# Double-to-single weight words: four VectorE steps or three, and where ScalarE's word lies

## Chip, core and metric

One NeuronCore of one Trainium2 chip. Its engines each take their own instructions in program order: TensorE (PE, matrix products, with a separate weight load PEld), VectorE (DVE), ScalarE (ACT), GpSimd (POOL) and SyncE (SP), which here issues almost all DMAs. Matrix products are written to PSUM, eight banks of 512 single-precision columns in each of 128 partitions; DVE and ACT read and write it. The metric is the device time of one execution in microseconds (us), the median of several runs.

## What is computed

Attention with hashed buckets, and a two-layer feed-forward part on its output:

```python
q_bits = (einsum('bhsd,dk->bhsk', q, proj) > 0)          # 6 hash bits, k the same
mask = q_bucket[:, :, :, None] == k_bucket[:, :, None, :]
scores = where(mask, matmul(q, k.T) / sqrt(D), -1e9)
attn = exp(scores - max(scores)); attn /= sum(attn) + 1e-9
x = matmul(attn, v)                  # 4 batches, 8 heads, 768 rows, 64 columns -> (3072, 512)
h = x @ w_in                         # (512, 2048)
g = where(h >= 1, h, where(h <= -1, 0, (h + 1) ** 2 / 4))
out = g @ w_out                      # (2048, 512)
```

`w_in` and `w_out` come in double precision. The kernel sees each weight as two 32-bit words (low and high) and has to make the single-precision word itself: the sign, the exponent with its bias changed, and the top 23 bits of the fraction, of which 20 lie in the high word and 3 at the top of the low word.

## The kernel before

**Heads, units, queues.** There are 32 heads in 16 pairs. A head has 12 units: six blocks of 128 keys for each half of the queries (384 columns). Unit g puts out two score products (L372, L373) into a PSUM bank "s", then two exponentials on ACT: `ph` (L381) and the same again unrounded (L386), in place or, for blocks 0 and 3, in the SBUF tile `pf`. The subtraction of the two (L392, recorded at line 39 of the helper `sub`) is done one unit later, on DVE or, for blocks 0 and 3, on POOL. Four units later three products (L405, L407, L409) add the unit to the output bank: `obank[0]` while the first half of the queries runs, `obank[1]` for the second. After a half's last block ACT copies the bank to SBUF (L415). So bank 0 takes products in units 4 to 9 of a head, bank 1 in units 10 to 15, that is, up to unit 3 of the next head.

**Row maxima.** Two heads ahead, PE forms the products of the row maxima, a pair of matmuls (L311) at the end of every second unit. DVE reduces both halves at once (L315) in the next unit. There is one such two-bank tile, so the next pair of matmuls waits for the reduction. POOL clamps the finished maxima (L343, L345), PE transposes them (L350), ACT copies them (L355) and two DMAs put them away.

**Hash bits.** For the pair after next, POOL rounds the raw queries and keys and subtracts (L153, L158) in units 0 to 3 of an even head. `bits_mm` forms a hash product of four matmuls (L211) for each half and ACT negates a part of it (L217); `bits_cmp`, one unit later, compares on DVE (L222). Line 589 says at which unit and in which bank; a DMA (`move`, part 3) and POOL's scaling (`bits_scale`) are set relative to the second product, the put of the bits at unit 18.

**Weight words.** `WeightSplit.steps` returns a word's steps as closures: a load of 128 x 512 doubles (`s0`), a square on ACT and a first DVE step (`s1`), three more DVE steps (`s2`, `s3`, `s4`), then a rounding (`s5`, L87 or L89), the remainder (`s6`, POOL or DVE, line 39) and DMAs (`put`, `get`). The last DVE step uses the square to set words to zero whose exponent is too small. `conv` hangs the steps of a word on the units of a head by a tuple of offsets. Twelve words of `w_in` start with every odd head from head 3 (L1166), twelve more words (four of `w_in`, eight of `w_out`) with every even head from head 4 (L1178). The eight left are made in the feed-forward part, by steps set a given number of blocks before the word is needed (L1234).

**Order.** Nothing is reordered: the loop over the units (L614 to L636) calls a unit's score products, the reduction held over, the subtraction of the unit before, the output products, and then the tasks hung on that unit. The feed-forward loop does the same with `prep` and `post`.

Of the kernel before, what the change touches and what calls it, by code (L numbers as in the profile page):

```python
# [31 lines left out]
BIG = 2.0 ** 36  # L32
CLAMP = 2.0 ** 33
SCALE = 1.0 / 8.0
WMIN2 = float(np.array([897 << 20], np.int32).view(np.float32)[0]) ** 2


def sub(nc, eng, out, a, b):
# [3 lines left out]
class WeightSplit:  # L42
# [3 lines left out]
    def __init__(self, nc, pool, n):  # L46
        self.nc, self.pool, self.n = nc, pool, n
        sc = pool.tile([P, 2], I32, name="wsc", bufs=1)
        nc.vector.memset(sc[:, 0:1], -0x40000000)
        nc.vector.memset(sc[:, 1:2], 29)  # L50
        self.sc = sc

    def steps(self, src, shape, hi, lo, cp, stage=None, low=None, keep=None):
        nc, n = self.nc, self.n
        st = {}

        def s0():
            st["raw"] = self.pool.tile([P, n, 2], I32, name="wraw")
            dst = st["raw"]
            if len(shape) == 4:  # L60
                dst = dst.rearrange("p (c f) t -> p c f t", c=shape[1])
            nc.sync.dma_start(out=dst, in_=src)

        def s1():
            raw = st["raw"]
            sq = st["sq"] = self.pool.tile([P, n], F32, name="wsq")
            a = st["a"] = self.pool.tile([P, n], I32, name="wa", bufs=1)
            high = raw[:, :, 1].bitcast(F32)
            nc.scalar.activation(out=sq, in_=high, func=AF.Square)
            nc.vector.tensor_scalar(out=a, in0=raw[:, :, 1], scalar1=0x07FFFFFF, scalar2=3,  # L70
                                    op0=ALU.bitwise_and, op1=ALU.logical_shift_left)

        def s2():
            nc.vector.scalar_tensor_tensor(out=st["a"], in0=st["raw"][:, :, 1], scalar=self.sc[:, 0:1],
                                           in1=st["a"], op0=ALU.bitwise_and, op1=ALU.bitwise_or)

        def s3():
            nc.vector.scalar_tensor_tensor(out=st["a"], in0=st["raw"][:, :, 0], scalar=self.sc[:, 1:2],
                                           in1=st["a"], op0=ALU.logical_shift_right, op1=ALU.bitwise_or)

        def s4():
            nc.vector.scalar_tensor_tensor(out=st["sq"], in0=st["sq"], scalar=WMIN2,
                                           in1=st["a"].bitcast(F32), op0=ALU.is_ge, op1=ALU.mult)

        def s5():
            if cp is nc.scalar:
                cp.copy(out=hi, in_=st["sq"])  # L87
            else:
                cp.tensor_copy(out=hi, in_=st["sq"])  # L89

        def s6():
            sub(nc, low or nc.gpsimd, lo, st["sq"], hi.bitcast(F32))

        def put():
            nc.sync.dma_start(out=keep if stage is None else stage, in_=st["sq"])

        if stage is None:
            return [s0, s1, s2, s3, s4, s5, s6] + ([put] if keep is not None else [])

        def get(sq=None):  # L100
            st["sq"] = self.pool.tile([P, n], F32, name="wsq") if sq is None else sq
            nc.sync.dma_start(out=st["sq"], in_=stage)

        return [s0, s1, s2, s3, s4, put], [get, s5, s6]


NQK, NV, NP_ = 3, 2, 7
# [7 lines left out]
def attention(ctx, tc, wst, T1, T2, qk, v, pj, cv, x_d, s_d, e_d, tasks, shared):  # L115
# [1 line left out]
    const = ctx.enter_context(tc.tile_pool(name="aconst", bufs=1))  # L117
    work = ctx.enter_context(tc.tile_pool(name="awork", bufs=2))
    small = ctx.enter_context(tc.tile_pool(name="asmall", bufs=2))
    shared["work"], shared["small"] = work, small  # L120
    ps_s = ctx.enter_context(tc.tile_pool(name="ps_s", bufs=4, space=PSUM))
    ps_o = ctx.enter_context(tc.tile_pool(name="ps_o", bufs=1, space=PSUM))
    ps_m = ctx.enter_context(tc.tile_pool(name="ps_m", bufs=1, space=PSUM))
# [447 lines left out]
    for hd in range(NH):  # L571
        pr, h = hd // 2, hd % 2
        g = hd * NU
        if 0 < hd < NH - 2:
            gc, gt = ((30, 33), (41, 43))[hd - 1] if hd < 3 else (g + NU + SHIFT - 1, g + NU + SHIFT + 1)
            at(gc, max_clamp, hd + 2, nc.gpsimd)
            at(gt, max_tr, hd + 2)
            at(gt, max_put, hd + 2)
        if h == 0 and pr + 2 < NPAIR:
            g0 = g + (13, 2)[pr] if pr < 2 else g  # L580
            for n in range(4):
                at(g0 + n, cast_h, pr + 2, nc.gpsimd, n % 2, n // 2)
                at(g0 + n, low_h, pr + 2, nc.gpsimd, n % 2, n // 2)
            at(g0 + 3, move, pr + 2, 0)
            at(g0 + 3, move, pr + 2, 1)
            at(g0 + 6, move, pr + 2, 2)
            if pr + 3 < NPAIR:
                at(g0 + 7, load_raw, pr + 3)
            bits_at = ((20, 1), (23, 0)) if pr == 0 else ((8 if pr == 1 else 7, 1), (11, 0))
            for hf, (n, bank) in enumerate(bits_at):  # L590
                at(g + n, bits_mm, pr + 2, hf, bank)
                at(g + n + 1, bits_cmp, pr + 2, hf)
            at(g + n + 1, move, pr + 2, 3)
            at(g + n + (2 if pr else 1), bits_scale, pr + 2, nc.gpsimd if pr else nc.scalar)
            at(g + (18 if pr else 25), bits_put, pr + 2)
        if h == 0 and pr + 1 < NPAIR:
            gv = g + LAG + (2 if pr else 16)
            at(gv, cast_v, pr + 1, nc.scalar)
            at(gv + 1, split_v, pr + 1, nc.gpsimd, 0)
            at(gv + 3, split_v, pr + 1, nc.gpsimd, 1)  # L600
            if pr + 2 < NPAIR:
                at(gv + (6 if pr else 4), load_v, pr + 2)
# [503 lines left out]
def lsh_attn_ffn(ctx: ExitStack, tc: tile.TileContext, qk, v, pj, cv, w_in, w_out, out):  # L1106
# [46 lines left out]
    def conv(g, steps, offs):  # L1153
        for fn, n in zip(steps, offs):
            at(g + n, fn)

    def wi_steps(i, cp, stage=None):
        return ws.steps(win_v[:, :, i * P:(i + 1) * P, :], (P, NCT, P, 2), wih[i], wil[i], cp, stage, None, wq[i])

    def wo_steps(i, cp, stage=None, low=None):  # L1160
        return ws.steps(wout_v[i], (P, DM, 2), woh[i], wol[i], cp, stage, low)

    woh = [hi for hi, lo in wo]
    wol = [lo for hi, lo in wo]
    for i in range(NW1):
        conv((2 * i + 3) * NU, wi_steps(i, nc.scalar), (0, 7, 9, 13, 15, 17, 19, 21))  # L1166
    g0 = (NH - 4) * NU
    late = {}
    for n in range(NSTG):
        i = n - (NFT - NW1)  # L1170
        stage = wq[NW1 + n] if i < 0 else xdp.tile([P, DM], F32, name=f"wd{n}")
        if i < 0:
            first, late[n] = wi_steps(NW1 + n, nc.vector, stage)
        elif i < 2:
            first, late[n] = wo_steps(i, nc.vector, stage)
        else:
            first, late[n] = wo_steps(i, nc.scalar, stage, nc.gpsimd if i < 4 else nc.vector)
        conv((4 + 2 * n) * NU, first, (0, 7, 9, 13, 15, 16))  # L1178
    for n, g in enumerate((1, 7, 13, 25, 30, 35)):
        conv(g0 + g, late[n], (0, 5, 6))  # L1180

    actx = ExitStack()
    attn = {}
    for b in range(B - 1):
        g = (b + 1) * H * NU + LAG + 4
        at(g, lambda b=b: xm.sums_load(*(attn["small"].tile([P, NF], F32, name=n, bufs=1) for n in ("sm", "em")), b))
# [31 lines left out]
    for i in range(2, NFT):  # L1218
# [12 lines left out]
        else:  # L1231
            need -= 2 + (i > 9)
            *st, cast, low = wo_steps(i, nc.scalar, None, nc.vector)
            for fn, m in zip(st, (6, 4, 4, 3, 3)):  # L1234
                prep[need - m].append((fn, ()))
            n_cast, n_low = need - 3, need - 2
        post[n_cast].append((cast, ()))
# [53 lines left out]
```

## Time and profile before

| | us |
|---|---|
| runs (3) | 979.09, 979.32, 982.97 |
| median | 979.32 |
| profiled execution | 979.4 |
| its span | 977.6 |
| DVE busy | 788.3 |
| ACT busy | 680.2 |
| POOL busy | 354.8 |

The span is what the profiler recorded between the first and the last instruction. The granted clock of PE is 0.9 of full speed or more in every slice. Busy times are sums over instructions; PE's matmuls are pipelined, so that two of them overlap in the record and a busy PE is not a PE at its peak: the distance between the starts of neighbours says more. An idle engine that nobody waits for costs nothing.

Slices 1 to 18 of the 40 are attention, the rest the feed-forward part. The busy shares in tenths:

```profile
PE   8999999999999999999999999999999999999998
PEld 7889999999999999999999998888988888888896
DVE  8779999999999999897898788787776777655554
```

### The profile page before, as it was taken

Reading aid. Unit: us, or ns where it says so; the run is one execution under the profiler, and the core shown is the slowest. Engines: PE = TensorE matmul, PEld = TensorE weight load, DVE = VectorE, ACT = ScalarE, POOL = GpSimd, SP = SyncE. Lnnn points to the kernel's source line nnn. Section 1 sums busy time; section 2 is a strip of 40 time slices with the busy share of each in tenths; the row PEclk is TensorE's granted clock in tenths of the full one; section 3 lists DMA queues with packets and bytes.
Section 4 is the critical chain, followed back from the end, with each engine's and each line's share of the span. In section 5 each row is a group of like instructions: output and inputs, shape, how many; then the busy total and the mean of one; then the engine's idle time right before and its main releaser. Section 6 shows DMA issues by size and latency. Waiting matters only on the chain.

```text
span 977.6 us, 15547 instructions
## 1 busy us (share of the span) xinstructions
PE 961.9 (98%) x5050; PEld 890.3 (91%) x5050; DVE 788.3 (81%) x1355; ACT 680.2 (70%) x1481; POOL 354.8 (36%) x422
## 2 busy tenths in 40 slices
PE   8999999999999999999999999999999999999998
PEld 7889999999999999999999998888988888888896
DVE  8779999999999999897898788787776777655554
ACT  7888998989989998987755565455564545544444
POOL 8768887777788877566000000000000000000000
PEclk9999999999999999999999999999999999999999
DMA  5775566677666666635494479976459554454431
GB/s 161 191 183 157 153 170 177 175 191 197 179 167 166 157 175 176 153 114 134 128 335 162 139 227 300 295 241 201 119 160 236 146 183 118 148 154 119 119 87 65
DMA packets 95113, 167.56 MB, mean 171 GB/s; under 512 B 13956, under 2 KB 51960, under 8 KB 95032
## 3 DMA queue, kind: packets, MB, share of 16 engines
q1 hardware_dynamic: 94808, 166.56, 60.7%
q8 instruction: 40, 0.66, 0.3%
q14 instruction: 41, 0.34, 0.1%
q10 hardware_dynamic: 224, 0.00, 0.0%
HBM read 106.13 MB, written 33.87 MB: 143 GB/s over the span
## 4 chain that ended last, share of the span: by engine, by line
PE 86%; DVE 5%; POOL 5%; ACT 1%; issue 1%; DMA 1%; DVEq 0%; POOLq 0%; ACTq 0%
PE y L829 27%; PE h L1061 18%; PE h L966 7%; PE smax L311 6%; PE s L373 5%; PE s L372 5%; PE o L405 5%; PE o L407 5%; PE o L409 5%; POOL t L39 3%; PE o L211 2%; DVE nm L315 2%; DVE pl L39 1%; POOL pl L39 1%; POOL t L153 1%
## 5 line engine op out<-in xcount | busy, mean ns | idle before, releaser
L381 ACT ACTIVATE ph<-s 128x384 fp32r<-128x384 f32 x380 | 188.6, 496 | 41.2 <-PE s L373 36.1
L315 DVE TENSOR_REDUCE nm<-smax 128x1 f32<-128x768 f32 x189 | 179.3, 949 | 22.2 <-PE smax L311 21.0
L39 POOL TENSOR_TENSOR pl<-pf,ph 128x384 fp32r<-128x384 f32 x128 | 134.1, 1052 | 78.8 <-ACT pf L386 78.8
L794 DVE SCALAR_TENSOR_TENSOR t<-t 128x384 f32<-128x384 f32 x128 | 71.2, 557 | 101.0 <-ACT z L789 100.8
L39 DVE TENSOR_TENSOR pl<-s,ph 128x384 fp32r<-128x384 f32 x256 | 135.4, 545 | 10.9 <-ACT s L386 9.0
L372 PE MATMUL s<-t 128*128 128x384 f32 x384 | 132.2, 344 | 0.0
L373 PE MATMUL s<-t 128*128 128x384 f32 x384 | 129.6, 337 | 1.7 <-DMA t<-te 1.7
L409 PE MATMUL o<-pl,va 128*128 128x386 f32 x384 | 130.4, 340 | 0.4 <-DVE pl L39 0.4
L407 PE MATMUL o<-ph,vb 128*128 128x386 f32 x384 | 130.0, 339 | 0.0
L405 PE MATMUL o<-ph,va 128*128 128x386 f32 x384 | 129.9, 338 | 0.0
L386 ACT ACTIVATE s<-s 128x384 f32<-128x384 f32 x252 | 125.5, 498 | 0.0
L829 PE MATMUL y<-t,ghi 128*128 128x512 f32 x384 | 124.7, 395 | 0.0
L311 PE MATMUL smax<-t 128*128 128x384 f32 x378 | 100.1, 346 | 4.5 <-DVE nm L315 4.4
L788 ACT ACTIVATE t<-h,mh 128x384 f32<-128x384 f32 x56 | 32.5, 581 | 82.2 <-PE h L966 43.5
L799 ACT CAST ghi<-z 128x384 fp32r<-128x384 f32 x129 | 65.1, 505 | 30.6 <-DVE z L795 26.9
L789 ACT ACTIVATE z<-t,m 128x384 f32<-128x384 f32 x128 | 79.0, 617 | 4.2
L829 PEld LDWEIGHTS y<-t,ghi 128*128 128x128 f32 x384 | 71.3, 188 | 11.1 <-ACT ghi L799 0.3
L1061 PE MATMUL h<-wbig,t 128*128 128x384 f32 x399 | 81.4, 336 | 0.0
L311 PEld LDWEIGHTS smax<-t 128*128 128x128 f32 x378 | 66.6, 188 | 14.5 <-DVE nm L315 13.7
L1061 PEld LDWEIGHTS h<-wbig,t 128*128 128x128 f32 x399 | 71.6, 188 | 5.2
L788 ACT ACTIVATE t<-wsq,mh 128x384 f32<-128x384 f32 x48 | 29.6, 617 | 66.7 <-DVE wsq L1074 40.4
L829 PE MATMUL y<-t,glo 128*128 128x512 f32 x192 | 76.0, 396 | 0.0
(190 smaller groups left out, 2142.9 us busy)
## 6 DMA issues: line engine op xcount, KB each, us to landing
t<-wc SPq DMA_DIRECT2D x92, 256.0 KB
t<-t SPq DMA_DIRECT2D x60, 384.0 KB
wraw<-wc SPq DMA_DIRECT2D x76, 256.0 KB
raw<-in_qk_dram SPq DMA_DIRECT2D x14, 768.0 KB
wraw<-in_w_in_dram SPq DMA_DIRECT2D x16, 512.0 KB
wraw<-in_w_out_dram SPq DMA_DIRECT2D x16, 512.0 KB
t<-ed SPq DMA_DIRECT2D x36, 192.0 KB
xd<-xs SPq DMA_DIRECT2D x32, 192.5 KB
```

Of the source, the lines that this page charges most:

```text
L39: eng.tensor_tensor(out=out, in0=a, in1=b, op=ALU.subtract)
L311: nc.tensor.matmul(out=smax[hd][:, hf, 0:HS], lhsT=t2[:, 0, h, i * P:(i + 1) * P], rhs=t2[:, 1, h, hf * HS:(hf + 1) * HS], start=True, sto ...
L315: nc.vector.tensor_reduce(out=nmp(hd)[:, i:i + 1], in_=smax[hd][:, :, 0:HS], axis=AX.XY, op=ALU.max, negate=True)
L372: nc.tensor.matmul(out=ps[:, 0:HS], lhsT=t1[:, 1, h, ks], rhs=t1[:, 0, h, sl], start=True, stop=False)
L373: nc.tensor.matmul(out=ps[:, 0:HS], lhsT=t2[:, 1, h, ks], rhs=t2[:, 0, h, sl], start=False, stop=True)
L381: nc.scalar.activation(out=ph[:, 0:HS], in_=ps[:, 0:HS], func=AF.Exp, scale=SCALE)
L386: nc.scalar.activation(out=pf, in_=ps[:, 0:HS], func=AF.Exp, scale=SCALE)
L405: nc.tensor.matmul(out=o, lhsT=wa, rhs=ph, start=(jj == 0), stop=False)
L407: nc.tensor.matmul(out=o, lhsT=wb, rhs=ph, start=False, stop=False)
L409: nc.tensor.matmul(out=o, lhsT=wa, rhs=pl, start=False, stop=(jj == NJ - 1))
L829: nc.tensor.matmul(out=ys[c][m], lhsT=g_[:, m * P:(m + 1) * P], rhs=w, start=(first and k == 0), stop=(last and k == 2))
L1061: nc.tensor.matmul(out=ps, lhsT=w[:, cs], rhs=x, start=(n == 0 and s not in (2, 3, 6)), stop=(n == 5), skip_group_check=True)
```

## The change

The square is gone. ACT multiplies the high word, read as a single-precision number, by 2^-112 (`rebias`); that changes the exponent's bias and lets too small numbers go to zero by itself. DVE shifts the low word right (`tail`), shifts ACT's word left by three and joins the two (`shifted`), and puts the sign back (`signed`): three steps instead of four. Where a word is made in attention, ACT writes its result into output bank 0 instead of SBUF, between that bank's copy at unit 9 and its next products; the other words use the SBUF tile that will hold the result. The two hash products of a pair go to units 5 and 7, both in bank 1, where they were at 7 (bank 1) and 11 (bank 0); the first two pairs keep theirs. The offsets of the steps change with it.

```diff
-WMIN2 = float(np.array([897 << 20], np.int32).view(np.float32)[0]) ** 2
+REBIAS = 2.0 ** -112
...
-        nc.vector.memset(sc[:, 0:1], -0x40000000)
-        nc.vector.memset(sc[:, 1:2], 29)
+        nc.vector.memset(sc[:, 0:1], 3)
+        nc.vector.memset(sc[:, 1:2], -0x80000000)
...
-        def s1():
-            raw = st["raw"]
-            sq = st["sq"] = self.pool.tile([P, n], F32, name="wsq")
+        def tail():
             a = st["a"] = self.pool.tile([P, n], I32, name="wa", bufs=1)
-            high = raw[:, :, 1].bitcast(F32)
-            nc.scalar.activation(out=sq, in_=high, func=AF.Square)
-            nc.vector.tensor_scalar(out=a, in0=raw[:, :, 1], scalar1=0x07FFFFFF, scalar2=3,
-                                    op0=ALU.bitwise_and, op1=ALU.logical_shift_left)
-
-        def s2():
-            nc.vector.scalar_tensor_tensor(out=st["a"], in0=st["raw"][:, :, 1], scalar=self.sc[:, 0:1],
-                                           in1=st["a"], op0=ALU.bitwise_and, op1=ALU.bitwise_or)
-
-        def s3():
-            nc.vector.scalar_tensor_tensor(out=st["a"], in0=st["raw"][:, :, 0], scalar=self.sc[:, 1:2],
-                                           in1=st["a"], op0=ALU.logical_shift_right, op1=ALU.bitwise_or)
-
-        def s4():
-            nc.vector.scalar_tensor_tensor(out=st["sq"], in0=st["sq"], scalar=WMIN2,
-                                           in1=st["a"].bitcast(F32), op0=ALU.is_ge, op1=ALU.mult)
+            nc.vector.tensor_scalar(out=a, in0=st["raw"][:, :, 0], scalar1=29, scalar2=None,
+                                    op0=ALU.logical_shift_right)
+
+        def rebias():
+            st["sq"] = self.pool.tile([P, n], F32, name="wsq")
+            g = st["g"] = st["sq"] if word is None else word()
+            nc.scalar.activation(out=g, in_=st["raw"][:, :, 1].bitcast(F32), func=AF.Copy, scale=REBIAS)
+
+        def shifted():
+            nc.vector.scalar_tensor_tensor(out=st["a"], in0=st["g"].bitcast(I32), scalar=self.sc[:, 0:1],
+                                           in1=st["a"], op0=ALU.logical_shift_left, op1=ALU.bitwise_or)
+
+        def signed():
+            nc.vector.scalar_tensor_tensor(out=st["sq"].bitcast(I32), in0=st["g"].bitcast(I32),
+                                           scalar=self.sc[:, 1:2], in1=st["a"], op0=ALU.bitwise_and,
+                                           op1=ALU.bitwise_or)
...
-    shared["work"], shared["small"] = work, small
+    shared["work"], shared["small"], shared["word"] = work, small, lambda: obank[0]
...
-            bits_at = ((20, 1), (23, 0)) if pr == 0 else ((8 if pr == 1 else 7, 1), (11, 0))
+            bits_at = (((20, 1), (23, 0)), ((8, 1), (11, 0)))[pr] if pr < 2 else ((5, 1), (7, 1))
...
-        conv((2 * i + 3) * NU, wi_steps(i, nc.scalar), (0, 7, 9, 13, 15, 17, 19, 21))
+        conv((2 * i + 3) * NU, wi_steps(i, nc.scalar), (0, 7, 9, 10, 13, 15, 17, 19))
...
-        conv((4 + 2 * n) * NU, first, (0, 7, 9, 13, 15, 16))
+        conv((4 + 2 * n) * NU, first, (0, 7, 9, 10, 13, 14))
...
-            for fn, m in zip(st, (6, 4, 4, 3, 3)):
+            for fn, m in zip(st, (6, 4, 4, 4, 3)):
```

The lists of steps that `steps` returns name the new closures in the order load, `tail`, `rebias`, `shifted`, `signed`; `wi_steps` passes `word` always, `wo_steps` only in attention.

More of the change, by code (lines that the diff above doesn't have):

```diff
@@ L48, in __init__, with steps @@
         sc = pool.tile([P, 2], I32, name="wsc", bufs=1)
-        nc.vector.memset(sc[:, 0:1], -0x40000000)
-        nc.vector.memset(sc[:, 1:2], 29)
+        nc.vector.memset(sc[:, 0:1], 3)
+        nc.vector.memset(sc[:, 1:2], -0x80000000)
         self.sc = sc
-    def steps(self, src, shape, hi, lo, cp, stage=None, low=None, keep=None):
+    def steps(self, src, shape, hi, lo, cp, stage=None, low=None, keep=None, word=None):
         nc, n = self.nc, self.n
@@ L97, in steps @@
         if stage is None:
-            return [s0, s1, s2, s3, s4, s5, s6] + ([put] if keep is not None else [])
+            return [s0, tail, rebias, shifted, signed, s5, s6] + ([put] if keep is not None else [])
         def get(sq=None):
@@ L102, in get @@
             nc.sync.dma_start(out=st["sq"], in_=stage)
-        return [s0, s1, s2, s3, s4, put], [get, s5, s6]
+        return [s0, tail, rebias, shifted, signed, put], [get, s5, s6]
 NQK, NV, NP_ = 3, 2, 7
@@ L1155, in conv, with word @@
             at(g + n, fn)
+    attn = {}
+    def word():
+        return attn["word"]()
     def wi_steps(i, cp, stage=None):
-        return ws.steps(win_v[:, :, i * P:(i + 1) * P, :], (P, NCT, P, 2), wih[i], wil[i], cp, stage, None, wq[i])
+        return ws.steps(win_v[:, :, i * P:(i + 1) * P, :], (P, NCT, P, 2), wih[i], wil[i], cp, stage, None, wq[i], word)
     def wo_steps(i, cp, stage=None, low=None):
-        return ws.steps(wout_v[i], (P, DM, 2), woh[i], wol[i], cp, stage, low)
+        return ws.steps(wout_v[i], (P, DM, 2), woh[i], wol[i], cp, stage, low, None, None if stage is None else word)
     woh = [hi for hi, lo in wo]
@@ L1182, in lsh_attn_ffn @@
     actx = ExitStack()
-    attn = {}
     for b in range(B - 1):
```

## The prediction, made before the changed kernel was run

> **What bounds the kernel now.** First the page: who is busy, and how long the span is.
>
> ```profile
> span 977.6 us, 15547 instructions
> ...
> PE 961.9 (98%) x5050; PEld 890.3 (91%) x5050; DVE 788.3 (81%) x1355; ACT 680.2 (70%) x1481; POOL 354.8 (36%) x422
> ```
>
> TensorE (PE) is busy 98% of 977.6 us; the execution took 979.4 us, and the median of the three runs is 979.32, so a sum made on this execution carries over unchanged. Next the busy time by stretch (columns: window, its length, PE, PE's weight loads, VectorE (DVE), ScalarE (ACT), GpSimd (POOL), granted clock, DMA share, GB/s). I cut it at 62 us, where head 3 begins with the first weight word's load, at 402 us, after the last word made in attention, and around the feed-forward part.
>
> ```profile
> 62.00:402.00 340.00, 334.75 (x1879) 324.44 (x1879) 317.12 (x472) 305.52 (x730) 264.94 (x292) 1.00 0.67 174
> ...
> 461.00:968.00 507.00, 506.94 (x2524) 455.80 (x2524) 368.58 (x714) 270.35 (x511) 2.54 (x2) 1.00 0.59 175
> ```
>
> From 461 to 968 us PE is idle for 0.06 us. Eight of the 32 words are made there; nothing they save can shorten it. The other 24 lie between 62 and 402 us, where DVE works 317 of 340 us and ACT 306. What can be won is what PE loses there. The waits of that stretch (us in total, times, longest):
>
> ```profile
> PEld smax L311 <- DVE nm L315: 7.5, 19, 0.8
> ...
> PEld s L350 <- POOL nm L345: 4.3, 8, 0.6
> ```
>
> Two causes, 19 and 8 times. Their price is read from the starts of PE in the timeline (start, us, engine, line, work, idle before): two neighbouring matmuls start 0.175 us apart when nothing is late.
>
> ```profile
> 77.06 0.33 PE L373 MATMUL s<-t 128*128 128x384 f32 x1
> 77.88 0.63 PE L311 MATMUL smax<-t 128*128 128x384 f32 x2 [0.49 <-DVE nm L315]
> ...
> 90.01 0.62 PE L311 MATMUL smax<-t 128*128 128x384 f32 x2
> ...
> 105.48 0.34 PE L409 MATMUL o<-pl,va 128*128 128x386 f32 x1
> 105.81 0.62 PE L311 MATMUL smax<-t 128*128 128x384 f32 x2
> ...
> 111.20 0.34 PE L409 MATMUL o<-pl,va 128*128 128x386 f32 x1
> 111.73 0.28 PE L350 MATMUL s<-ident,nm 128*12 128x128 f32 x1 [0.19 <-POOL nm L345]
> ...
> 162.93 0.45 PE L409 MATMUL o<-pl,va 128*128 128x386 f32 x1
> 163.80 0.62 PE L311 MATMUL smax<-t 128*128 128x384 f32 x2 [0.42 <-DVE nm L315]
> ...
> 394.94 0.62 PE L311 MATMUL smax<-t 128*128 128x384 f32 x2
> ```
>
> The pair of row-max products (L311) after 105.48 starts 0.33 later, so 0.15 us is lost. Fifteen losses are of this short kind: 11 at a pair's first unit (as here), four in an even head (the first and the last, 90.01 and 394.94, are shown). Four are long: 0.82 − 0.175 = 0.65 at 77.88, and 0.87 − 0.175 = 0.70 at 163.80, which returns for each of three batches. The transpose L350 at 111.73 starts 0.53 after its neighbour: 0.36 lost, eight times. In all 15 × 0.15 + 0.65 + 3 × 0.70 + 8 × 0.36 = 7.9 us. That is the whole prize, 0.8%.
>
> Why are these late? VectorE, then GpSimd, around 105 us:
>
> ```profile
> 103.35 1.54 DVE L74 SCALAR_TENSOR_TENSOR wa<-wraw,wsc,wa 128x512 int32<-128x512 int32 x1
> 104.81 0.94 DVE L315 TENSOR_REDUCE nm<-smax 128x1 f32<-128x768 f32 x1
> ...
> 107.47 0.84 DVE L78 SCALAR_TENSOR_TENSOR wa<-wraw,wsc,wa 128x512 int32<-128x512 int32 x1
> ...
> 110.02 1.25 DVE L82 SCALAR_TENSOR_TENSOR wsq<-wsq,wa 128x512 f32<-128x512 f32 x1
> ```
>
> ```profile
> 104.28 0.97 POOL L153 CAST t<-raw 128x384 fp32r<-128x384 f32 x1
> ...
> 107.84 1.34 POOL L39 TENSOR_TENSOR t<-raw,t 128x384 fp32r<-128x384 f32 x1
> 109.13 0.50 POOL L153 CAST t<-raw 128x384 fp32r<-128x384 f32 x1
> 109.71 1.02 POOL L39 TENSOR_TENSOR t<-raw,t 128x384 fp32r<-128x384 f32 x1
> 110.69 0.67 POOL L343 TENSOR_SCALAR nm<-nm 128x6 f32<-128x6 f32 x1
> 111.45 0.23 POOL L345 TENSOR_SCALAR nm<-nm 128x6 f32<-128x6 f32 x1
> ```
>
> The long step L74 (1.54 us) ends at 104.89; the max reduction L315 follows, ends at 105.75, and PE's next row-max pair, due at 105.66, waits for it. On POOL the cast of 0.97 us lies beside L74, the subtraction of 1.34 beside L78, and the clamp of 0.67 beside L82; elsewhere on POOL the same cast takes 0.50 and the same subtraction 1.02. The clamp's second half ends at 111.69; the transpose was due at 111.20 + 0.175 = 111.38.
>
> **The change part by part.**
>
> ```profile
> L74 DVE SCALAR_TENSOR_TENSOR wa<-wraw,wsc,wa 128x512 int32<-128x512 int32 x24 | 27.6, 1149 | 0.0
> L82 DVE SCALAR_TENSOR_TENSOR wsq<-wsq,wa 128x512 f32<-128x512 f32 x24 | 21.3, 889 | 0.0
> L78 DVE SCALAR_TENSOR_TENSOR wa<-wraw,wsc,wa 128x512 int32<-128x512 int32 x24 | 20.9, 870 | 0.0
> ...
> L70 DVE TENSOR_SCALAR wa<-wraw 128x512 int32<-128x512 int32 x24 | 13.3, 556 | 0.1
> ```
>
> *DVE.* Four steps of 1.15, 0.89, 0.87 and 0.56 us, 3.47 per word, become three. The shift of the low word has the form and place of L70: 0.56. The other two read one operand from PSUM and one from SBUF, which no step here does with this operation; the nearest rows:
>
> ```profile
> L39 DVE TENSOR_TENSOR pl<-s,ph 128x384 fp32r<-128x384 f32 x195 | 102.7, 543 | 3.9 <-ACT s L386 3.7
> ```
>
> ```profile
> L39 DVE TENSOR_TENSOR wbig<-pcs,wbig 128x384 fp32r<-128x384 f32 x30 | 16.2, 550 | 0.0
> ...
> L39 DVE TENSOR_TENSOR wol<-wsq,woh 128x512 fp32r<-128x512 f32 x8 | 5.5, 684 | 0.0
> ```
>
> A two-operand step from PSUM takes 543 ns on 384 columns, 550 with both in SBUF (second row); 512 columns take 684 (third). Bounds for the new steps: 0.54 (384 columns) and 1.15 (L74's mean, if they are held up as L74 is). I take 0.70, just above the 684, since the 195 steps from PSUM show no hold-up beside a busy POOL. Per word 0.56 + 2 × 0.70 = 1.96: 1.5 us less, 36 us over 24 words. None of this is the gain: PE waits only where DVE is late.
>
> [...]
>
> *POOL.* L82 at the clamp and L78 at the subtraction are replaced by one PSUM step, at the pair's second unit, and nothing at its fourth. Without them the subtraction falls from 1.34 to 1.02 and the clamp from 0.67 to the 0.23 of its second half: 0.76 us sooner, 110.93 instead of 111.69, before 111.38. (The cast's 0.47 I count at nothing: POOL then waits for ACT.) All eight transpose waits go: **−2.9 us**. POOL could still be held up by PSUM steps; bounds 0 and −2.9, and I take the lower by the PSUM rows.
>
> *ACT and the new wait.* The square (0.66 us, 7 units after the load) becomes a scaled copy, 9 units after it, right behind the copy of the output bank.
>
> ```profile
> 101.04 0.66 ACT L69 ACTIVATE wsq<-wraw 128x512 f32<-128x512 f32 x1
> ...
> 103.11 0.50 ACT L415 COPY xs<-o 128x384 f32<-128x384 f32 x1
> ```
>
> The bank copy starts at 103.11 and is over at 103.60; the next can start a little before. The scaled copy of 512 columns is bounded by 0.49 (the bank copy, 384 columns) and 0.66 (the square, the same source); I take 0.66 from 103.5: it ends near 104.15. The DVE step behind it stands one unit later in the program; DVE is free at 103.35 and must wait, with the reduction L315 queued behind it, for which PE's row-max pair waits. 104.15 + 0.70 = 104.85, against 104.89 before. So the short loss at the odd head's word stays, 0.15, for another reason: first DVE was slow, now it waits for ACT. **0.**
>
> At 77.88 DVE was later than usual; the copy is tied to PE, so that loss falls from 0.65 to 0.15: **−0.5.**
>
> The three batch losses come from the sums' step:
>
> ```profile
> 161.49 0.92 DVE L674 TENSOR_SCALAR sm<-sm 128x48 f32<-128x48 f32 x1
> ```
>
> ```profile
> L674 DVE TENSOR_SCALAR pcs<-pcs 128x48 f32<-128x48 f32 x1 | 0.2, 189 | 0.0
> ```
>
> It takes 0.92 us beside a busy POOL; the same form takes 189 ns where POOL rests (second row). If POOL's earlier order leaves it free, most of 0.70 goes; if not, none. Between 0 and −2.1 I take half: **−1.0.**
>
> *Hash products.* Four matmuls each, at units 7 and 11 of an even head before, now at 5 and 7, both in bank 1.
>
> ```profile
> 111.76 0.42 PE L372 MATMUL s<-t 128*128 128x384 f32 x1
> ...
> 113.94 0.86 PE L211 MATMUL o<-t,pw 128*128 128x384 f32 x4
> ```
>
> ```profile
> 115.97 0.55 DVE L222 TENSOR_TENSOR neg<-o,neg 32x384 f32<-32x384 f32 x1 [0.47 <-ACT neg L217]
> ```
>
> One product costs PE 4 × 0.175 = 0.70 us, wherever it stands. Three consequences. The first product, due after the transpose at about 111.5, needs POOL's second subtraction: ended by 109.18, no wait. The second overwrites what the first's compare reads: from product to compare's end were 113.94 to 116.52, 2.6 us; the new distance is 0.70 + (113.94 − 111.76) = 2.9, and the 0.66 square has left that chain. No wait; margin 0.3 to 0.9. Third, the product at unit 11 stood between two row-max pairs and gave DVE 0.70 us more there. Without it an even head's word is as an odd one's, with a short loss: 12 words, of which four lose now, so 8 × 0.15 = **+1.2.**
>
> *Moved DMAs and POOL work.* On SyncE's queue the move behind the hash goes four units sooner, the put of the word two: they pass bank-row writes and a load that PE needs a whole head later; neither is among the causes counted above. The hash's scaling on POOL goes before a subtraction wanted five units on. Casts of a finished word, two units sooner, meet ACT behind a bank copy, when PE has four units in hand. **0.** If that cover is gone, they belong to the ACT rival.
>
> Sum: −2.9 − 0.5 − 1.0 + 1.2 = −3.2; 979.4 − 3.2 = **976.2 us.**
>
> **The rivals.**
> 1. *POOL's waits stay* (the PSUM steps block it as L74 did, or the earlier PE finds it late anyway): 976.2 + 2.9 = 979.1. For: POOL waits for ACT's exponentials in these units, and ACT gets later. Against: the PSUM rows.
> 2. *The wait for the copy is hidden*, DVE being 1.5 us per word freer: all 7.9 us go, 971.5. Against: DVE stood ready at 103.35, 0.8 us before the copy ends, and takes its instructions in order.
> 3. *Slower: DVE held behind ACT.* Each 0.1 us that the copy ends later than 104.15 passes through two DVE instructions to PE, 24 times: 2.4 us. The forecast's gain is gone at 0.13 us; at 0.33 the kernel is over 0.5% slower. Were ACT late by one instruction such as the bank copy (0.49 us): 976.2 + 11.8 = 988.0. For: ACT is 90% busy. Against: nothing stands between the bank copy and the scaled one.
> 4. *Slower: the hash waits*, if POOL's second subtraction or the first compare comes late: 12 heads, 6 us for each 0.5 us; at 1 us, 988.2. Against: margins of 2.3 and 0.3 to 0.9.
> 5. *PSUM steps dearer*: if the step at 104.15 takes L78's 0.87 us, PE is 0.17 later 24 times: 4.1 us, 980.3. Against: 543 and 550 above. [...]
>
> **How the numbers follow.** Forecast 0.45; POOL's waits stay 0.22; PSUM dearer 0.05; all gone 0.15; DVE behind ACT 0.09; hash 0.04. About 0.5% (4.9 us) is what a measurement can tell from no change: 974.4 to 984.2 holds the forecast and rivals 1 and 5, so same 0.72, faster 0.15, slower 0.13. The range runs from 971.3, just below rival 2, to 983.9: rival 1, with the new step and the copy each 0.1 us dearer (979.1 + 4.8). It leaves out rivals 3 and 4 for the most part, and no more.
>
> **What would show it.** After: no transpose L350 waiting for POOL, POOL's cast at 0.50 and its subtraction at 1.02 throughout; two DVE steps near 0.70; DVE idle before the first of them, released by ACT's copy, in nearly every word; row-max waits some 20 times, all short; PE without idle from 461 us on. I am wrong if the new DVE steps exceed 0.85 us, if the copy starts more than half a microsecond after the bank copy's start, or if a hash product waits for POOL or for the compare.

## The result, and the profile after

The changed kernel takes 984.5 us (median of 22 runs, 980.08 to 990.65) where the kernel before takes 980.84 in 22 runs (978.86 to 983.4). The ratio is 1.0044, 95% interval 1.0031 to 1.0056: slower by 0.44%, at the edge of the 0.5% that a measurement was said to tell. The forecast was faster by 0.33% (976.2 against 979.4); the time is above the range's upper end of 983.9. The profiled execution took 983.81 us.

The page of the changed kernel, its span and engines, and the chain that ended last by engine:

```profile
span 982.0 us, 15544 instructions
...
PE 963.3 (98%) x5050; PEld 890.5 (91%) x5050; DVE 752.4 (77%) x1323; ACT 683.2 (70%) x1481; POOL 320.2 (33%) x422
...
PE 77%; DMA 8%; DVE 6%; ACT 4%; issue 2%; POOL 1%; SPq 0%; DVEq 0%; POOLq 0%; ACTq 0%
```

DVE works 35.9 us less and POOL 34.6 us less, as intended, and the span is 4.4 us longer. What is new is the DMA share, 8% of the chain. The same line of the page of before has 1%:

```profile
PE 86%; DVE 5%; POOL 5%; ACT 1%; issue 1%; DMA 1%; DVEq 0%; POOLq 0%; ACTq 0%
```

Next, the same stretches as before (window, its length, PE, PEld, DVE, ACT, POOL, clock, DMA share, GB/s):

```profile
62.00:402.00 340.00, 332.73 (x1861) 321.28 (x1860) 283.25 (x443) 306.19 (x725) 230.78 (x291) 1.00 0.68 173
...
461.00:968.00 507.00, 507.00 (x2530) 456.60 (x2529) 363.07 (x708) 270.00 (x513) 3.79 (x4) 1.00 0.59 176
```

The feed-forward part is full, as it was. In the stretch of the weight words DVE is 34 us freer, and PE is busy 2.0 us less of the same 340. The waits there (us in total, times, longest):

```profile
DVE wa L66 <- DMA wraw<-in_w_in_dram: 14.7, 11, 2.0
PEld smax L309 <- DVE nm L313: 12.5, 26, 0.7
DVE wa L75 <- ACT o L72: 12.4, 16, 0.9
...
PEld s L348 <- POOL nm L343: 0.2, 1, 0.2
```

(Lines have moved: row-max pair L311 is now L309, its reduction L315 is L313, the transpose L350 is L348. New are DVE's L66, L75 and L79 and ACT's L72.) The transposes' waits are all but gone (0.2 us, once). In their place stand two new waits of DVE: its first step for the word's load, its second for ACT's copy. PE on one odd-head word and one even-head word:

```profile
104.47 0.44 PE L407 MATMUL o<-pl,va 128*128 128x386 f32 x1 [0.23 <-DVE pl L39]
105.34 0.62 PE L309 MATMUL smax<-t 128*128 128x384 f32 x2 [0.42 <-DVE nm L313]
...
121.51 0.34 PE L407 MATMUL o<-pl,va 128*128 128x386 f32 x1
122.00 0.62 PE L309 MATMUL smax<-t 128*128 128x384 f32 x2
```

By the starts, as in the prediction: 0.87 − 0.175 = 0.70 us lost at 105.34, 0.49 − 0.175 = 0.31 at 122.00. An even head's word always costs about 0.31; six of the odd heads' words cost 0.63 to 0.70. ACT, then DVE, ahead of the short loss at 122.00, and DVE ahead of the next long one, at 133.66:

```profile
119.66 0.64 ACT L72 ACTIVATE o<-wraw 128x512 f32<-128x512 f32 x1
```

```profile
120.33 0.75 DVE L75 SCALAR_TENSOR_TENSOR wa<-o,wsc,wa 128x512 int32<-128x512 int32 x1 [0.88 <-ACT o L72]
121.00 0.95 DVE L313 TENSOR_REDUCE nm<-smax 128x1 f32<-128x768 f32 x1
...
131.85 0.43 DVE L66 TENSOR_SCALAR wa<-wraw 128x512 int32<-128x512 int32 x1 [1.82 <-DMA wraw<-in_w_in_dram]
132.19 0.55 DVE L39 TENSOR_TENSOR pl<-s,ph 128x384 fp32r<-128x384 f32 x1
132.66 0.95 DVE L313 TENSOR_REDUCE nm<-smax 128x1 f32<-128x768 f32 x1
```

At 131.85 DVE has stood for 1.82 us with its queue blocked by a word step that nobody needs yet. Behind it wait a subtraction and the reduction, and for these PE. The chain that leads there (start, us, what):

```profile
117.40 4.27 DMA t<-t
...
122.27 9.48 DMA wraw<-in_w_in_dram
```

and SyncE's queue around it, first of the changed kernel, then of the one before:

```profile
118.00 0.54 SPq L93 DMA_DIRECT2D wq<-wsq  x1
118.59 1.37 SPq L146 DMA_DIRECT2D raw<-in_qk_dram  x1
121.75 0.47 SPq L162 DMA_DIRECT2D t<-t  x1
122.27 0.58 SPq L62 DMA_DIRECT2D wraw<-in_w_in_dram  x1
```

```profile
116.87 0.59 SPq L148 DMA_DIRECT2D raw<-in_qk_dram  x1
117.56 1.34 SPq L95 DMA_DIRECT2D wq<-wsq  x1
118.94 0.45 SPq L62 DMA_DIRECT2D wraw<-in_w_in_dram  x1
120.43 0.47 SPq L164 DMA_DIRECT2D t<-t  x1
```

Two things changed places. The hash's last `move` (the `t<-t` row) now stands ahead of the word's load, and it waits for the move before it to land, 4.27 us from 117.40: the load goes out at 122.27, 3.3 us later than before. Of these, 1.75 us are lost by the whole kernel by then (DVE was ready for the word at 131.85 − 1.82 = 130.03, before at 128.28); against DVE the load is 1.6 us late. And the put of the last word (`wq<-wsq`) stands ahead of the 768 KB load of raw queries and keys instead of behind it. The word's load then takes 9.48 us to land; the load of 118.94 in the kernel before took 7.34 (how a landing is counted is said at the runs on the puts).

### The profile page after: what moved, and what is told of

Its sections match the earlier page's. It is cut to its first block, busy times and chain, and to the rows that moved or that the text cites. A ratio compares the mean times of both kernels' runs of the same rounds, so it can differ in the third digit from the quotient of the medians.

```text
span 982.0 us, 15544 instructions
## 1 busy us (share of the span) xinstructions
PE 963.3 (98%) x5050; PEld 890.5 (91%) x5050; DVE 752.4 (77%) x1323; ACT 683.2 (70%) x1481; POOL 320.2 (33%) x422
## 4 chain that ended last, share of the span: by engine, by line
PE 77%; DMA 8%; DVE 6%; ACT 4%; issue 2%; POOL 1%; SPq 0%; DVEq 0%; POOLq 0%; ACTq 0%
PE y L827 27%; PE h L1059 18%; PE h L964 7%; PE smax L309 5%; DMA wraw<-in_w_in_dram 5%; PE s L371 4%; PE s L370 4%; PE o L405 4%; PE o L403 4%; PE o L407 4%; DVE nm L313 3%; DMA t<-t 2%; DMA t<-te 2%; PE o L209 1%; ACT ph L379 1%
## 5 line engine op out<-in xcount | busy, mean ns | idle before, releaser
L313 DVE TENSOR_REDUCE nm<-smax 128x1 f32<-128x768 f32 x189 | 179.9, 952 | 35.6 <-PE smax L309 33.7
L309 PE MATMUL smax<-t 128*128 128x384 f32 x378 | 100.8, 348 | 7.5 <-DVE nm L313 5.3
L309 PEld LDWEIGHTS smax<-t 128*128 128x128 f32 x378 | 66.1, 188 | 19.2 <-DVE nm L313 18.3
L407 PEld LDWEIGHTS o<-pl,va 128*128 128x128 f32 x384 | 72.6, 189 | 4.0 <-DVE pl L39 3.8
```

Source lines behind the costliest of these rows:

```text
L309: nc.tensor.matmul(out=smax[hd][:, hf, 0:HS], lhsT=t2[:, 0, h, i * P:(i + 1) * P], rhs=t2[:, 1, h, hf * HS:(hf + 1) * HS], start=True, sto ...
L313: nc.vector.tensor_reduce(out=nmp(hd)[:, i:i + 1], in_=smax[hd][:, :, 0:HS], axis=AX.XY, op=ALU.max, negate=True)
L407: nc.tensor.matmul(out=o, lhsT=wa, rhs=pl, start=False, stop=(jj == NJ - 1))
```

## The experiments

The queue theory: the loss comes from DMAs that the change moved on SyncE's queue. Its main rival: it comes from the new wait for ACT's copy, or from the new steps themselves. The first runs tell these apart; the later ones tell which DMA it is.

**The moved `move`.** In the first kernel the hash's last move goes back to unit 12, behind the word's load. In the second it stays and every word's load goes out four units earlier; in the third all but the first word's.

```diff
-            at(g + n + 1, move, pr + 2, 3)
+            at(g + (12 if pr > 1 else n + 1), move, pr + 2, 3)      # e1
-  wi_steps(i, nc.scalar), (0, 7, 9, 10, 13, 15, 17, 19))
+  wi_steps(i, nc.scalar), (-4, 7, 9, 10, 13, 15, 17, 19))           # e2, the even heads alike
+  wi_steps(i, nc.scalar), (-4 if i else 0, 7, 9, 10, 13, 15, 17, 19))  # e5
```

> The changed kernel with the fourth move of a pair back at unit 12 of the even head, behind the word load of the odd head in SyncE's queue. Theory Q (queue): at unit 8 this move waits for the third move to land, and the odd head's word load stands behind it and comes 3.3 us later than before; DVE's first step then waits for the load (14.7 us in 11 waits) and PE's row-max pair waits for DVE. Q expects DVE's waits for the word load to fall under 2 us and the time to lie 0.2 to 0.5% under the changed kernel, at 0.998 to 1.002 of the kernel before. Theory W (the step behind ACT's copy holds DVE, and PE loses there): the load waits may go but the time stays, 1.003 to 1.005.

Measured: 0.9997 (0.9985 to 1.0008). The waits for the load fall from 14.7 us to 3.8, not under 2 as expected, and the loss of time against the kernel before is gone. The wait for ACT's copy stays (18.3 us), so it alone doesn't make the kernel slower than before.

> The changed kernel with every attention word's load four units sooner, the fourth move left at unit 8. Q expects the same as from the move put back: DVE's waits for the word load under 2 us, 0.998 to 1.002 of the kernel before. If the fourth move itself were the cost (for what it does to other transfers and not through the word load), the time would stay at 1.003 to 1.005.

Measured: 1.0046 (1.0033 to 1.0059), which the queue theory did not expect, although the waits for the load fell to 3.9 us here too. The trace shows a loss of another kind, once: the first word's load had gone ahead of the small DMA that brings PE the row maxima of head 3 (`t<-te`), and PE stood for 4.93 us, in the changed kernel 1.93. The third kernel leaves that first load where it was.

> The changed kernel with every attention word's load four units sooner except the very first, whose load then stays behind the row transfer that PE waits for at 62 us; the fourth move left at unit 8. Theory Q (the word load is held in SyncE's queue behind the fourth move) expects what the move put back gave, 0.998 to 1.001 of the kernel before, with the wait at 62 us back under 2.5 us and the clock full there. If the fourth move costs in another way, 1.003 to 1.005.

Measured: 0.9997 (0.9984 to 1.0009), load waits 3.7 us. So an earlier load does what the move back does.

**The wait for ACT's copy.** The two-operand step moves from unit 10 to 11, with the move back (e3) and without it (e6); then e3 again with ACT's word in SBUF (e7).

```diff
-  (0, 7, 9, 10, 13, 15, 17, 19)
+  (0, 7, 9, 11, 13, 15, 17, 19)        # e3, e6, e7; the even heads alike
-            g = st["g"] = st["sq"] if word is None else word()
+            g = st["g"] = st["sq"]       # e7
```

> The fourth move back at unit 12 and, besides, the first step that reads ACT's word one unit later (11 instead of 10). Theory W expects DVE's 12.4 us of waits for ACT's copy to fall under 3 us and PE's short waits for the reduction in even heads (0.3 us each, 12 of them) to go: 3 to 5 us under the kernel with the move alone put back, 0.993 to 0.997 of the kernel before. Q alone expects no more than from the move alone.

> The changed kernel with only the first step that reads ACT's word one unit later, the fourth move left at unit 8. If queue and step add up: 3 us under the changed kernel, 0.999 to 1.003 of the kernel before, DVE's waits for ACT's copy gone and its waits for the word load still over 10 us. If the step alone explains the loss: 0.994 to 0.997.

> The fourth move back, the step one unit later, and ACT's word in SBUF, so that both steps have two SBUF operands. Theory P (it is the PSUM operand that keeps DVE and POOL out of each other's way) expects steps of 0.85 us and more, POOL's casts and clamps longer again, the transposes' waits for POOL back (some 8 of 0.3 us) and 2 to 6 us over the kernel with the word in PSUM: 0.998 to 1.002 of the kernel before. If one step fewer is all that helps: 0.995 to 0.997.

Measured: e3 0.9958 (0.9944 to 0.9972), e6 1.0052 (1.0034 to 1.007), e7 0.9976 (0.9962 to 0.9989). The later step takes the waits for ACT away in all three. With the move back that is worth 0.39% (0.9997 to 0.9958, about 3.8 us); with the load late nothing of it shows (e6 against the changed kernel's 1.0044, where 0.999 to 1.003 was expected): the waits for the load are 16.7 us in e6, and behind most of them PE still loses some 0.7 us. The word in PSUM may be worth some 0.18% (e3 to e7), but the intervals overlap. Groups of e3 and then of e7 in the stretch 62 to 402 (busy us, mean ns, idle before):

```profile
L39 POOL TENSOR_TENSOR t<-raw,t 128x384 fp32r<-128x384 f32 x48 | 48.8, 1017 | 3.9
L75 DVE SCALAR_TENSOR_TENSOR wa<-o,wsc,wa 128x512 int32<-128x512 int32 x24 | 17.8, 742 | 0.0
```

```profile
L39 POOL TENSOR_TENSOR t<-raw,t 128x384 fp32r<-128x384 f32 x48 | 52.7, 1097 | 3.9
L75 DVE SCALAR_TENSOR_TENSOR wa<-wsq,wsc,wa 128x512 int32<-128x512 int32 x24 | 19.5, 812 | 0.0
```

With both operands in SBUF the step takes 70 ns more on the mean and POOL's subtraction 80 ns more. The traces of the two main kernels point the same way. Before, L74 has both operands in SBUF and POOL busy beside each of its 24 steps: they take 0.73 to 1.57 us, and POOL is held up too (1.57 at 352.47, POOL's cast beside it 0.96; 0.73 at 117.77, the two POOL subtractions around it 2.74 together). In the changed kernel POOL is as busy beside the 24 steps of L75, which take 0.74 to 0.75 us, and the POOL subtractions beside them 1.00 to 1.03. e7 differs from e3 in the place of ACT's word alone; that its longer steps grow by POOL's work beside them is inferred from these rows, not shown. The shortest of e7's 24 steps takes 741 ns and the longest 926; in e3 they take 740 and 744. So for this step reading from PSUM is neither dearer nor cheaper in itself.

**Parts of the change alone.** The kernel before with the hash products at units 5 and 7, their last move and POOL's scaling following (e4); the same with the scaling held at unit 13 (e8); and the three new steps alone, with the step at unit 11 and the word in SBUF, the hash where it was (e11).

```diff
-            bits_at = ((20, 1), (23, 0)) if pr == 0 else ((8 if pr == 1 else 7, 1), (11, 0))
+            bits_at = (((20, 1), (23, 0)), ((8, 1), (11, 0)))[pr] if pr < 2 else ((5, 1), (7, 1))   # e4, e8
-            at(g + n + (2 if pr else 1), bits_scale, pr + 2, nc.gpsimd if pr else nc.scalar)
+            at(g + (13 if pr else n + 1), bits_scale, pr + 2, nc.gpsimd if pr else nc.scalar)       # e8
```

> The kernel before with only the hash products moved to units 5 and 7 in one bank (the fourth move follows them to unit 8); four DVE steps as before. Q expects the loss to be in this part: the odd head's load is late here too, DVE's first step waits for it by over 10 us in total, and the kernel is slower than before by 0.4 to 1.0%. If the new steps are what costs, this is 0.999 to 1.002.

Measured: 1.0167 (1.0152 to 1.0182), by a route that was not expected: no wait for a load at all. DVE's old four-step word and POOL meet instead. DVE, then POOL, in an even head of this kernel:

```profile
151.54 2.57 DVE L74 SCALAR_TENSOR_TENSOR wa<-wraw,wsc,wa 128x512 int32<-128x512 int32 x1
```

```profile
150.63 0.98 POOL L274 TENSOR_SCALAR bits<-neg,cvt 32x768 fp32r<-32x768 f32 x1
151.59 1.00 POOL L39 TENSOR_TENSOR vb<-vraw,va 128x384 fp32r<-128x384 f32 x1
```

The scaling, four units earlier, pushes two POOL subtractions (at 151.59 and 152.56) beside L74, which has both operands in SBUF: it takes 2.57 us, where its mean in the kernel before is 1.15 (0.73 to 0.88 in even heads), and PE waits 1.44 us for the reduction behind it. With the new steps the earlier scaling is cheap, and not only because of the operand in PSUM: in e7 it stands as early and both operands lie in SBUF, but the step comes two units later than L74 does here, its longest is 926 ns, and the kernel takes 0.9976. Whether the place or the number of the steps makes the difference wasn't tried apart. The prediction did not see that scaling and steps belong together.

> The kernel before with the hash products moved, but POOL's scaling of the bits left at unit 13. Theory: what cost 16 us when the hash was moved alone is POOL's scaling at unit 9, which puts POOL's subtractions beside the step L74 (1.92 us on the mean there). It expects L74 back at 1.2 us or less, the waits of 1.6 us in even heads gone, and 0.999 to 1.005 of the kernel before. If the cover that the second product gave DVE is what is missing: 1.012 to 1.018.

Measured: 1.0006 (0.9993 to 1.0018). With the scaling back, the moved hash costs nothing that can be measured, **though its word load also goes out late**: DVE waits for it 1.3 us in all. The move alone is therefore not enough. This kernel lacks the new steps and the earlier puts.

> The three new steps with ACT's word in SBUF, the step one unit later, and the hash products (with move and scaling) where they were. If the hash products' new place costs nothing once the fourth move is back: the same as with them moved and the word in SBUF, 0.996 to 0.999. If the second product's old place was worth something to DVE: 0.990 to 0.995.

Measured: 0.9976 (0.9963 to 0.9989), with 10.5 us of waits for the load (8 times) although the move stands where it stood before. It has the early puts, which points at these.

**The puts.** The changed kernel with both puts back at units 21 and 16 (e9), with the odd heads' alone (e13), with the even heads' alone (e14).

```diff
-  wi_steps(i, nc.scalar), (0, 7, 9, 10, 13, 15, 17, 19)
+  wi_steps(i, nc.scalar), (0, 7, 9, 10, 13, 15, 17, 21)    # e9, e13
-  first, (0, 7, 9, 10, 13, 14)
+  first, (0, 7, 9, 10, 13, 16)                              # e9, e14
```

> The changed kernel with only the words' puts back at their old units (21 in odd heads, 16 in even ones), the fourth move left at unit 8. The hash products alone, with the fourth move at unit 8 too, left DVE only 1.3 us of waits for the word load, so the queue theory has two forms. If the fourth move alone holds the load: load waits stay over 10 us and the time at 1.003 to 1.006. If the put that now stands in front of the raw load is needed too: load waits under 5 us and 0.998 to 1.001.

Measured: 0.9999 (0.9987 to 1.001), no wait for a load left. (Its profiled execution lost some 2 us at 62 us, last section.)

> The changed kernel with only the odd head's put of the word back from unit 19 to unit 21, behind the 768 KB raw load instead of directly ahead of it; the even head's put stays two units early, the fourth move stays at unit 8. If the put ahead of the raw load makes the word load slow: DVE's first step waits for the load under 4 us in all (14.7 in the changed kernel), ratio 0.998 to 1.001. If the even head's put does: waits 10 to 15 us, ratio 1.003 to 1.006. If both are needed or share it: in between, 1.001 to 1.003.

> The changed kernel with only the even head's put of the word back from unit 14 to unit 16; the odd head's put stays two units early, ahead of the raw load, and the fourth move stays at unit 8. If the put ahead of the raw load makes the word load slow: waits of DVE's first step for the load stay 10 to 15 us in all, ratio 1.003 to 1.006. If the even head's put does: under 4 us, ratio 0.998 to 1.001. If they share it: in between.

Measured: e13 0.998 (0.9966 to 0.9993) with 0.5 us of waits; e14 1.0025 (1.0007 to 1.0043) with 12.3 us. It is the odd heads' put. SyncE's queue of e13, and DVE's first step on the word that the last row loads:

```profile
115.69 1.87 SPq L146 DMA_DIRECT2D raw<-in_qk_dram  x1
119.23 0.46 SPq L162 DMA_DIRECT2D t<-t  x1
119.79 0.53 SPq L93 DMA_DIRECT2D wq<-wsq  x1
120.36 1.26 SPq L62 DMA_DIRECT2D wraw<-in_w_in_dram  x1
```

```profile
127.63 0.51 DVE L66 TENSOR_SCALAR wa<-wraw 128x512 int32<-128x512 int32 x1
```

The load waits for the move as in the changed kernel, but DVE reads the word 7.27 us behind the load's issue without a wait, where the changed kernel's load takes 9.48 us. In e14, put ahead, the load issued at 120.25 takes 8.05 us.

In the traces such a load raises its semaphore sixteen times, and a step that waits for it starts 0.1 us behind the sixteenth; that one counts here as the landing (e13: sixteen between 124.95 and 127.34, so 6.98 us from the issue). By it, the medians of eleven odd heads' words (all but the first), with the sum of DVE's waits for all 24; DVE is ready when it would have started the step without a wait for the load:

| kernel | last move | odd put | issue to DVE ready (us) | issue to landing (us) | waits (us) |
|---|---|---|---|---|---|
| before | unit 12 | behind raw load | 9.3 | 7.7 | 0.1 |
| e12 | unit 12 | behind | 9.1 | 7.5 | 0.3 |
| e13 | unit 8 | behind | 7.5 | 7.0 | 0.5 |
| e1 | unit 12 | ahead | 9.5 | 9.5 | 3.8 |
| e14 | unit 8 | ahead | 7.7 | 8.5 | 12.3 |
| changed | unit 8 | ahead | 7.7 | 8.9 | 14.7 |

The move's place sets how far ahead of DVE the load goes out, the put's how long the load takes; e8 and e9 (move at 8, put behind: 7.0 and 6.4, 7.5 and 6.4) and e11 (move at 12, put ahead: 9.1 and 9.9) fall in with these. The raw load, directly behind the early put, is slowed as well: its median landing is 6.6 us in the kernel before and in e13, 9.4 in e14 and 9.8 in the changed kernel. Why a put ahead of it does so isn't shown.

**Better versions.** e10 is e3 with the loads four units earlier, but for the first; e12 is e3 with both puts back; e15 is the changed kernel with only two offsets altered, the odd heads' put at 21 and the step at 11.

> The fourth move back, the step one unit later, and every attention word's load but the first four units sooner. With the move back the load waits are 4.9 us in 6 cases; these should go. If PE was waiting behind some of them: 1 to 2 us under the kernel without the sooner loads, 0.993 to 0.996 of the kernel before; if they were covered: 0.995 to 0.997.

> The changed kernel with the fourth move back at unit 12, both puts of the word back where they were (units 21 and 16) and the two-operand step one unit later (unit 11). The new DVE steps, ACT's word in the output bank and the hash products stay. Theory Q (the loss comes from the queue moves alone): DVE waits for the word's load under 2 us in all, no wait of the step for ACT's copy, and about what e3 gave without its last load waits (4.9 us of waits): ratio 0.991 to 0.996, 972 to 977 us. Rival S (the puts do not matter once the move is back): the load waits stay near 5 us and the ratio is that of e3, 0.994 to 0.997. Rival B (the changed kernel finds another bound): 0.998 or more.

> The changed kernel with two offsets undone or moved: the odd head's put of the word back from unit 19 to 21, and the two-operand step from unit 10 to 11. The fourth move stays at unit 8 and the even head's put at 14. Theory T (these two are the whole of the loss): DVE's waits for the load under 2 us, none for ACT's copy, and the ratio of e12, 0.992 to 0.997 (974 to 979 us). Rival M (the fourth move at unit 8 still costs on its own): above 0.998, with waits for a load or for the sent rows that e12 has not. Rival A (the step's later place gives nothing without the move back, as in e6): the ratio of e13, 0.997 to 0.9995.

Measured: e10 0.9944 (0.9923 to 0.9964), e12 0.9942 (0.993 to 0.9955), e15 0.9942 (0.9924 to 0.996). All three beat both kernels, by 0.6% the one before, and cannot be told apart. The waits of e15 in the stretch 62 to 402:

```profile
PEld smax L309 <- DVE nm L313: 3.4, 12, 0.7
PEld s L348 <- POOL nm L343: 2.7, 8, 0.3
...
DVE wa L66 <- DMA wraw<-in_w_in_dram: 1.0, 4, 0.4
```

With the two edits nothing is left of the loss against the kernel before: the move at unit 8 and the even heads' put may stay.

## Why the prediction was wrong

**Right: what is removed.** The transposes wait once, 0.2 us, not eight times. POOL's subtraction takes 1.02 us (1016 ns) as forecast, and its cast and DVE's new steps are near their 0.50 and 0.70. Groups of the changed kernel, 62 to 402 us:

```profile
L151 POOL CAST t<-raw 128x384 fp32r<-128x384 f32 x48 | 24.2, 504 | 0.0
...
L75 DVE SCALAR_TENSOR_TENSOR wa<-o,wsc,wa 128x512 int32<-128x512 int32 x24 | 17.9, 747 | 12.4 <-ACT o L72 12.4
L79 DVE SCALAR_TENSOR_TENSOR wsq<-o,wsc,wa 128x512 int32<-128x512 int32 x23 | 17.0, 739 | 0.0
```

The rivals "POOL's waits stay" and "PSUM steps dearer" did not come about. With a PSUM operand the step is not slower than with SBUF (742 ns in e3, 812 in e7; 740 and 741 the shortest). The batch losses of 0.70 went altogether, −2.1 where −1.0 was taken. The hash products wait for nothing: in e8 they cost nothing.

**Mis-sized: the short loss behind ACT's copy.** The prediction kept it at 0.15 ("So the short loss at the odd head's word stays, 0.15") and gave the even heads the same. It is 0.30. The mechanism was right (DVE waits for ACT in nearly every word), two durations were not: the copy starts 0.52 us behind the bank copy's start (119.14 to 119.66), not 0.39, and the step takes 0.75, not 0.70. That is 0.18 us, against which the copy itself took 0.02 less than the 0.66 assumed. 24 × 0.15 = 3.6 us. The 0.39 stood for a start while the copy still runs, and where ACT's word goes to SBUF (e7) that is what happens, at 0.36; into the bank that the copy reads, the start comes only when the copy has ended. The prediction had named a start more than half a microsecond behind as a sign of being wrong, and it came. This is the rival "DVE held behind ACT" in small, by its own price of 2.4 us for each 0.1 us. Moved one unit on, the step loses none of it, but some of the gain goes back to the transposes, which the earlier PE finds late again (2.0 us of waits in e3, 2.7 in e15): 3.8 us net.

**Failed: "Moved DMAs and POOL work … 0".** The prediction saw that the move and the put pass "bank-row writes and a load that PE needs a whole head later; neither is among the causes counted above". It doesn't say which load: the move passed the word's, the put the raw one. For both PE's need is beside the point: DVE's first step needs the word seven units after the load's place in the program, and PE's reductions stand behind that step in DVE's queue. The trace of before had the slack to read: the load issued at 118.94 (above), its step without a wait at

```profile
128.28 0.51 DVE L70 TENSOR_SCALAR wa<-wraw 128x512 int32<-128x512 int32 x1
```

which is 9.3 us from issue to use, of which the load took 7.3. After, by the table's medians, the load goes out 1.7 us less far ahead (9.3 to 7.7), which uses up the slack, and takes 1.2 us longer (7.7 to 8.9): 1.2 us short in the median, 14.7 us in 11 waits. The first half could be read from the queue's order; the longer landing could not be read from the trace of before. None of the rivals had this wait.

**The sum as it came out.** ACT's copies of the output bank, 64 in each trace, mark the same work in both kernels. The seventh and the 55th, ahead of the first late word and behind the last, of before and then of after:

```profile
75.20 0.49 ACT L415 COPY xs<-o 128x384 f32<-128x384 f32 x1
...
408.07 0.49 ACT L415 COPY xs<-o 128x384 f32<-128x384 f32 x1
```

```profile
76.24 0.49 ACT L413 COPY xs<-o 128x384 f32<-128x384 f32 x1
...
412.02 0.49 ACT L413 COPY xs<-o 128x384 f32<-128x384 f32 x1
```

Between them lie 332.87 us before and 335.78 after: 2.9 us lost, where the forecast gains 3.2. In e13, where one load is late by 0.5 us, the same two copies start at 74.76 and 407.11, 332.35 us apart, 0.5 less than before. So the copy's wait and the batches make +2.5 (3.6 − 1.05 more than forecast; −3.2 + 2.5 = −0.7, measured −0.5), and the late load makes 3.4 (335.78 − 332.35). The rest of the profiled execution's 4.4 us lies outside: 1.0 us ahead of 75 us, where PE waited 1.43 us at 54.84 for `t<-te` as the execution of before did not, and 0.5 behind 412. These are of one execution and need not be in the medians; the runs of the changed kernel spread over 10.6 us, those of before over 4.5. By the ratios the odd put back is worth 0.64% (1.0044 to 0.998), some 6 us, and by the profiled executions 4.6 (983.81 to 979.2); the difference isn't explained.

**Limits that hid each other.** Undone singly, the move (e1) ends most of the load's waits and the put (e13) nearly all, and either is enough to bring the time back to the kernel before; with the move in its old place and the put early, 3.8 us (e1) to 10.5 us (e11) of waits are left. With neither undone, the step's later place shows nothing (e6); with the put undone it is worth 0.4% (e13 to e15).

## What to carry to other kernels

When a step with DMAs is moved, write out the issuing queue's order before and after, and for each load that is passed take its slack (from landing to first use) and the instruction that uses it: on an engine that works in order, as DVE here (it stood 1.82 us at 131.85, and the reduction behind it began at 132.66), the price is that of whatever stands queued behind the use, not of the loaded data's last consumer. When a wait moves from one producer to another, ask when the new one is done and place the step behind it; here a place one unit later was worth 0.4%. If an edit gains nothing, try it again with the next limit removed before it is dropped.

## What the runs showed of the hardware

- **The landing time of a load went with what was queued well ahead of it.** The same 512 KB load landed after 7.0 us in the median (e13), 8.9 (changed kernel) and 8.5 (e14), by whether a 256 KB write stood ahead of a 768 KB load or behind it, while the word's load itself came behind both.
- **A row of the chain need not be a landing.** The chain of e13 has a row of 4.93 us for the word's load; it ends where an exponential starts that doesn't use the word, at the sixth of the load's sixteen signals. The last came 2.05 us later.
- **ScalarE's write into the bank that it has just read** starts 0.52 us after the start of a 0.49 us copy (the changed kernel's 119.14 and 119.66; the same in e3); with SBUF as the target it starts 0.36 us after the same copy (e7, the rows below), while the copy still runs. The exponential behind the scaled copy, of another bank, starts 0.56 us after that one's start although it takes 0.64. Whether the chip or a wait in the program holds the write into the bank isn't shown.

```profile
118.91 0.49 ACT L413 COPY xs<-o 128x384 f32<-128x384 f32 x1
119.27 0.69 ACT L72 ACTIVATE wsq<-wraw 128x512 f32<-128x512 f32 x1
```

- **A short PE wait can come with nearly half the granted clock, and need not.** Rows from 62 to 68 us, of the changed kernel (PE waited 1.93 us there) and of e9 (1.86 us):

```profile
62.00:68.00 6.00, 4.07 (x24) 3.75 (x23) 2.80 (x5) 2.94 (x8) 2.64 (x4) 1.00 0.83 235
```

```profile
62.00:68.00 6.00, 4.19 (x15) 4.19 (x16) 1.58 (x4) 2.05 (x5) 1.98 (x2) 0.72 0.85 248
```

The clock column is 1.00 in the first and 0.72 in the second, where neighbouring matmuls stood 0.30 to 0.32 us apart from the wait's end at 63.81 to 67.31, and 0.17 to 0.18 apart before the wait and from 67.75 on. In e2, after 4.93 us, the six microseconds from 68 had 0.51. Why one wait came with a lower clock and another of about its length without isn't shown. The lower clock is a loss of one place and some 2 us, and it blurs comparisons of single executions.
